# Warm-up matmuls as two half-row matmuls into the two banks of one PSUM tile

## The chip, the cores and the metric

The kernel runs on one core of one Trainium2 chip. The metric is the device time in microseconds. The time before is 263.78 us, the median of two runs (263.33 and 264.23). PE stands for TensorE, DVE for VectorE, ACT for ScalarE, POOL for GpSimd and SP for SyncE.

## The reference

A linear attention with cosine weights, followed by an MLP mixer over tokens and channels. There are 8 batches of 8 heads, 576 tokens and 64 elements per head; a model row is 512 wide.

```python
def _attn_ref(q, k, v):                       # (8, 8, 576, 64) each
    theta = np.pi / 2.0 * pos / S
    def phi(x, c, s):
        r = np.maximum(x, 0.0)
        return np.concatenate([r * c, r * s], axis=-1)
    q_p = phi(q, cos_w, sin_w)
    k_p = phi(k, cos_w, sin_w)
    kv = np.einsum('bhsf,bhsd->bhfd', k_p, v)
    z = np.sum(k_p, axis=2)
    num = np.einsum('bhsf,bhfd->bhsd', q_p, kv)
    den = np.einsum('bhsf,bhf->bhs', q_p, z)[..., None] + 1e-06
    return (num / den).astype(np.float32)

def _moe_ref(x, w_tok1, w_tok2, w_ch1, w_ch2):    # x: (8, 576, 512)
    xt = x.transpose(0, 2, 1)
    h = np.maximum(xt @ w_tok1, 0.0) @ w_tok2     # 576 -> 256 -> 576
    u = x + h.transpose(0, 2, 1)
    h2 = np.maximum(u @ w_ch1, 0.0) @ w_ch2       # 512 -> 1536 -> 512
    return (u + h2).astype(np.float32)
```

The warm-up matmuls are no part of this. They multiply zeros by zeros, and nobody reads what they write.

## The kernel before, in words

The work is one long list, PLAN, which a loop at L877 walks through. Each entry names a function and its arguments, and the function issues its instructions on the engine that the entry names ("V" VectorE, "A" ScalarE, "G" GpSimd, "Y" the SP queue). The order on every engine is therefore the order of the list, written out by hand; nothing rearranges it later. An instruction waits by semaphore for the instructions whose results it reads, or whose tile it overwrites.

A batch goes through these steps. `load_part` brings q, k and v in. `feat` and `rfeat` (L382, L384, L400, L402) make the features on ScalarE and VectorE: relu, times a cosine, sine or tangent. `vcast` casts v. PE then transposes the features of q (`q_half_mm` and `q_turn_mm`, L688 and L702; the copies out are `q_half_out` and `q_turn_out`, L376 or L378), or the DMA engines do it (L414). `kv` and `kv_half` (L601, L715) multiply the features of k with v, `num` and `num_half` (L619, L729) the features of q with that product. VectorE divides (`x_add`, `x_rec`, `x_mul` and their halves, L633 to L647 and L737 to L744). `b1` (L657, L754) and `u_mm` (L766; for batch 0 `uT_x` and `uT_h`, L669 and L674) are the two token layers, and `u_out` (L770) adds x. Then `m1` (L809) is the first channel layer. The second one is `m2` (L821) for batch 0 and, for the other batches, seven products of half-size blocks (L454) with sums of their operands made beforehand (L437, L443). Batch 0 runs in halves of four heads while its inputs still arrive. Batches overlap: while `m1` of one runs, the features of the next are made.

PSUM is cut into six tiles (L482): two named psA of two banks each (kind "P") and four named psM of one bank (kind "S"). `take(kind, key)` (L487) takes the tile that has stood longest in the list of free ones, and `give(key)` (L492) puts it back at the end. Both act when the list is walked, so a tile can be taken again while its last reader has yet to run; the next writer then waits for that reader.

`warm(n)` (L588) issues n matmuls of the tile `wz` (L359, 128 rows of 512 bfloat16 zeros, set by VectorE at L501) on a tile taken and given back at once. PLAN holds 28 calls `("warm", 2)`, thus 56 matmuls: 13 calls before the first transposes of q, 12 more until the token layers of batch 0 are under way, one each in the first and the second channel layer of batch 0, and one behind the last product.

Before each matmul PE loads its stationary operand with an LDWEIGHTS of its own (PEld in the profile), here `wz[:, 0:P]`.

Of the kernel before, what the change touches and what calls it, by code (L numbers as in the profile page):

```python
# [285 lines left out]
def kernel(  # L286
# [11 lines left out]
    nc = tc.nc  # L298

    B, H, S, D = q.shape  # L300
# [3 lines left out]
    P = 128  # L304
# [16 lines left out]
    def sb(name, shape, dt):  # L321
        return const.tile(shape, dt, name=name)
# [36 lines left out]
    wz = sb("wz", [P, 512], BF16)  # L359
# [124 lines left out]
    free = {n: list(range(len(t))) for n, t in tiles.items()}  # L484
    held = {}

    def take(kind, key):  # L487

        held[key] = (kind, free[kind].pop(0))
        return tiles[kind][held[key][1]]  # L490

    def give(key):  # L492
        kind, i = held.pop(key)
        free[kind].append(i)
# [91 lines left out]
        copy(eng, wc2[:, ki, :], wc2_st[ki // 4][:, ki % 4, :])  # L586

    def warm(n):  # L588
        ps = take("S", "warm")
        for _ in range(n):  # L590
            nc.tensor.matmul(ps, wz[:, 0:P], wz, start=True, stop=True)  # L591
        give("warm")


# [315 lines left out]
```

## Time and profile before

| | |
|---|---|
| median of two runs | 263.78 us (263.33 to 264.23) |
| the profiled execution, its own time | 263.85 us |
| its span | 262.1 us |
| granted TensorE clock | 1.00 |
| chain that ended last, by engine | PE 71%, DMA 11%, DVE 10%, ACT 3% |
| warm-up matmuls (L591), share of that chain | 2% |
| HBM | 35.85 MB read, 9.44 MB written |

The profile is that of one execution. The span goes from the first to the last instruction, and the time of the execution is 1.75 us longer. A matmul's duration goes from its start to the modelled end of its pipeline, so successive matmuls overlap, and PE can read as busy while it waits briefly. In a row of the page, `L591 PE MATMUL psM<-wz 128*128 128x512 bf16 x56` is a line of the kernel, the engine and operation, tile written and tile read, rows and columns of the stationary operand, the shape of the moving one, and the number of such instructions; behind the bar stand the busy time in us, the mean duration of one in ns, and the idle time ahead of them with its releaser. A row of the timeline begins with its start and its length in us, and merges like neighbours. In the chain of waits each piece has its start, its length and the work that the end waited for.

### The profile page before, as it was taken

How to read it: one execution, taken by the hardware profiler on the slowest of the kernel's cores; microseconds unless marked ns; L12 is line 12 of the kernel's file. 1: busy time of each engine (PE TensorE's matmuls, PEld its weight loads, DVE VectorE, ACT ScalarE, POOL GpSimd, SP SyncE). 2: the span in 40 equal slices, each digit the busy share in tenths (PEclk: the TensorE clock that was granted, in tenths of full speed). 3: DMA queues.
4: the chain of work that ended last, by engine and by line, in shares of the span. 5: the costliest groups of instructions: out<-in, count | busy, mean ns of one | idle time of the engine just before them, and what ended most of it. 6: DMA issues, size and time to landing. Idle time of an engine off the chain costs nothing.

```text
span 262.1 us, 5484 instructions
## 1 busy us (share of the span) xinstructions
PE 254.6 (97%) x2122; PEld 160.5 (61%) x2122; DVE 193.0 (74%) x401; ACT 134.9 (51%) x226; POOL 89.3 (34%) x97
## 2 busy tenths in 40 slices
PE   8999989998999999999999999999999999999995
PEld 2576446445559556765577557755866586467684
DVE  4686996596999677797989878787878283634673
ACT  2794677593676388566743675374621442240100
POOL 5262372249413002930260038005701630073040
PEclk9999999999999999999999999999999999999999
DMA  6999999999999999999999999798392130400224
GB/s 189 383 389 386 386 347 313 328 229 185 325 396 197 220 265 388 186 227 252 368 268 163 251 314 275 163 304 136 72 170 93 51 75 8 141 1 0 99 104 160
DMA packets 81819, 57.70 MB, mean 220 GB/s; under 512 B 50305, under 2 KB 76545, under 8 KB 81793
## 3 DMA queue, kind: packets, MB, share of 16 engines
q1 hardware_dynamic: 80272, 55.65, 78.6%
q10 hardware_dynamic: 1520, 1.70, 1.9%
q8 instruction: 16, 0.26, 0.4%
q14 instruction: 11, 0.08, 0.1%
HBM read 35.85 MB, written 9.44 MB: 173 GB/s over the span
## 4 chain that ended last, share of the span: by engine, by line
PE 71%; DMA 11%; DVE 10%; ACT 3%; issue 2%; POOL 1%; ACTq 0%; SPq 0%; DVEq 0%; POOLq 0%
PE psM L809 26%; PE psM L454 22%; DMA q_raw<-in_q_dram 5%; PE psA L754 5%; PE psA L766 4%; DMA k_raw<-in_k_dram 3%; PE psA L729 3%; PE psA L715 2%; DMA uT<-u_bf 2%; PE psM L591 2%; DVE kp L402 2%; PE psM L821 2%; ACT kp L400 2%; DMA qpT<-qp 2%; DVE qp L402 1%
## 5 line engine op out<-in xcount | busy, mean ns | idle before, releaser
L809 PE MATMUL psM<-uT,w_ch 128*128 128x512 bf16 x384 | 90.2, 379 | 0.8 <-DMA uT<-u_bf 0.8
L382 ACT ACTIVATE h1T<-psM 128x512 bf16<-128x512 f32 x71 | 40.9, 595 | 68.9 <-PE psM L809 63.8
L809 PEld LDWEIGHTS <-w_ch 128*128 128x128 bf16 x432 | 40.2, 98 | 41.8 <-DMA uT<-u_bf 0.9
L454 PEld LDWEIGHTS <-h1s 128*128 128x128 bf16 x384 | 36.9, 98 | 8.1 <-POOL h1s L443 0.8
L384 DVE TENSOR_SCALAR h1T<-psM 128x512 bf16<-128x512 f32 x37 | 25.1, 686 | 16.6 <-PE psM L809 10.6
L466 DVE TENSOR_TENSOR u_sb<-psM,u_sb 128x512 f32<-128x512 f32 x42 | 28.1, 682 | 11.9 <-PE psM L454 11.5
L443 POOL TENSOR_TENSOR h1s<-h1T,h1s 128x512 bf16<-128x512 bf16 (+1 forms) x17 | 27.4, 1621 | 23.4 <-DVE h1s L443 17.1
L378 POOL CAST vb<-v_raw 128x512 bf16<-128x512 f32 (+1 forms) x23 | 13.5, 618 | 61.2 <-DMA v_raw<-in_v_dram 48.6
L454 PE MATMUL psM<-w_ch2t,h1s 128*128 128x256 bf16 x276 | 33.6, 273 | 0.5 <-POOL h1s L443 0.5
L454 PEld LDWEIGHTS <-h1T 128*128 128x128 bf16 x288 | 27.9, 98 | 5.3
L443 POOL TENSOR_TENSOR h1s<-h1T 128x512 bf16<-128x512 bf16 (+1 forms) x11 | 17.7, 1616 | 31.8 <-DVE h1T L384 16.8
L454 PE MATMUL psM<-w_ch,h1T 128*128 128x256 bf16 x192 | 23.6, 273 | 0.0
L770 DVE TENSOR_TENSOR u_sb<-psA,x_sb 128x1024 f32<-128x1024 f32 x16 | 19.3, 1219 | 3.8 <-PE psA L766 3.7
L744 DVE TENSOR_TENSOR x_sb<-psA,rden 128x512 bf16<-128x512 f32 x28 | 18.9, 686 | 0.7
L400 ACT ACTIVATE qp<-q_raw,tan_t 128x512 bf16<-128x512 f32 (+1 forms) x25 | 16.2, 673 | 4.9 <-DMA q_raw<-in_q_dram 4.1
L400 ACT ACTIVATE kp<-k_raw,sin_t 128x512 bf16<-128x512 f32 (+1 forms) x24 | 15.7, 663 | 5.6 <-PE psA L715 4.5
L591 PE MATMUL psM<-wz 128*128 128x512 bf16 x56 | 16.9, 434 | 1.2 <-DVE wz L501 1.2
L729 PEld LDWEIGHTS <-qpT 128*128 128x128 bf16 x280 | 12.5, 98 | 6.3 <-DMA qpT<-qp 0.9
L376 ACT CAST u_bf<-u_sb 128x1024 bf16<-128x1024 f32 x10 | 10.4, 1044 | 10.6 <-DVE u_sb L770 8.6
L766 PE MATMUL psA<-B,w_tok 128*128 128x512 bf16 x64 | 15.6, 379 | 0.1
L754 PE MATMUL psA<-x_sb,w_tok 128*128 128x512 bf16 x56 | 14.5, 379 | 0.2 <-DVE x_sb L744 0.2
L400 ACT ACTIVATE kp<-k_raw,cos_t 128x512 bf16<-128x512 f32 (+1 forms) x22 | 14.5, 673 | 0.2 <-DMA k_raw<-in_k_dram 0.2
(124 smaller groups left out, 345.3 us busy)
## 6 DMA issues: line engine op xcount, KB each, us to landing
out_dram<-u_sb SPq DMA_DIRECT2D x32, 256.0 KB, 4.2
k_raw<-in_k_dram SPq DMA_DIRECT2D x7, 640.0 KB, 7.3
q_raw<-in_q_dram SPq DMA_DIRECT2D x7, 640.0 KB, 6.6
v_raw<-in_v_dram SPq DMA_DIRECT2D x7, 640.0 KB, 8.5
k_raw<-in_k_dram SPq DMA_DIRECT2D x7, 512.0 KB, 7.4
q_raw<-in_q_dram SPq DMA_DIRECT2D x7, 512.0 KB, 5.5
v_raw<-in_v_dram SPq DMA_DIRECT2D x7, 512.0 KB, 6.6
u_sb<-in_moe_w_ch_dram SPq DMA_DIRECT2D x2, 1024.0 KB, 9.1
```

What stands on the lines that cost most here:

```text
L382: eng.activation(out_ap, in_ap, AF.Relu)
L384: eng.tensor_relu(out_ap, in_ap)
L400: eng.activation(dst, src, AF.Relu, bias=0.0, scale=s)
L443: eng.tensor_tensor(out=o[:, k0:k1], in0=a[:, k0:k1], in1=b_[:, k0:k1], op=op)
L454: nc.tensor.matmul(bank[:, t * HC:(t + 1) * HC], lhs[:, ki, t * P:(t + 1) * P], rhs[:, ki, :], start=(first and ki == 0 and t == 0), stop= ...
L466: V.tensor_add(u, bank2(bank)[:, ts, :], u)
L591: nc.tensor.matmul(ps, wz[:, 0:P], wz, start=True, stop=True)
L729: nc.tensor.matmul(ps[:, h // HH, (h % HH) * E1:(h % HH + 1) * E1], qpT[:, h, j, :], kv_sb[:, h, 0:E1], start=True, stop=True, skip_group_ ...
L754: nc.tensor.matmul(ps[:, mi, :], w1[:, j, mi * P:(mi + 1) * P], rhs, start=(j == 0), stop=(j == NJ - 1))
L766: nc.tensor.matmul(ps[:, half, :], w2[:, ki, 2 * c + half, :], B1[b % 2][:, ki, :], start=(ki == 0), stop=(ki == NT - 1))
L770: V.tensor_add(u_sb[b % 2][:, 2 * c:2 * c + 2, :], of(("u", b, c)), x_sb[:, 2 * c:2 * c + 2, :])
L809: nc.tensor.matmul(ps.rearrange("p (t k) -> p t k", k=P), wc1[:, ki, s * P:(s + 1) * P], src[:, :, ki, :], start=(ki == 0), stop=(ki == NC ...
```

## The change

A call of `warm` looks whether a psA tile is free. If one is, the call takes it, and each of its matmuls becomes two: the first on rows 0 to 63 of `wz` into the tile's first bank, the second on rows 64 to 127 into its second bank. Both are 512 columns wide. If none is free, the call does as before. Matmuls of the computation itself keep their 128 rows, and the list PLAN is the same.

```diff
     def warm(n):
-        ps = take("S", "warm")
+        two = len(free["P"]) > 0
+        ps = take("P" if two else "S", "warm")
         for _ in range(n):
-            nc.tensor.matmul(ps, wz[:, 0:P], wz, start=True, stop=True)
+            if two:
+                for i, p0 in enumerate((0, P // 2)):
+                    nc.tensor.matmul(ps[:, i, :], wz[p0:p0 + P // 2, 0:P], wz[p0:p0 + P // 2, :], start=True, stop=True)
+            else:
+                nc.tensor.matmul(ps, wz[:, 0:P], wz, start=True, stop=True)
         give("warm")
```

Lines behind it move down by five: L688 becomes L693, L809 becomes L814.

## The prediction

> **What bounds the kernel now.** I read the page first: who is busy, and what a warm-up matmul costs.
>
> ```profile
> span 262.1 us, 5484 instructions
> ...
> PE 254.6 (97%) x2122; PEld 160.5 (61%) x2122; DVE 193.0 (74%) x401; ACT 134.9 (51%) x226; POOL 89.3 (34%) x97
> ...
> L809 PE MATMUL psM<-uT,w_ch 128*128 128x512 bf16 x384 | 90.2, 379 | 0.8 <-DMA uT<-u_bf 0.8
> L809 PEld LDWEIGHTS <-w_ch 128*128 128x128 bf16 x432 | 40.2, 98 | 41.8 <-DMA uT<-u_bf 0.9
> ...
> L591 PE MATMUL psM<-wz 128*128 128x512 bf16 x56 | 16.9, 434 | 1.2 <-DVE wz L501 1.2
> ```
>
> PE is the bound, with little idle time anywhere. One matmul of 512 columns lasts 379 ns from start to end, but eight take 1.73 us in the chain below, so they follow each other every 216 ns and 163 ns of each is tail under the next. The 98 ns weight load lies beside a running matmul. Every PE row says 128*128: no half-row matmul occurs before.
>
> Next the timeline of PE, to see where the 56 warm-ups lie and what they hold up.
>
> ```profile
> 1.19 8.36 PE L591 MATMUL psM<-wz 128*128 128x512 bf16 x26 [1.19 <-DVE wz L501]
> 9.38 0.61 PE L688 MATMUL psM<-ident,qp 128*128 128x128 bf16 x8
> 9.83 1.03 PE L591 MATMUL psM<-wz 128*128 128x512 bf16 x4
> 10.99 1.02 PE L688 MATMUL psM<-ident,qp 128*128 128x128 bf16 x12
> ```
>
> In the first stage PE has nothing else to do. Its weight loads start 0.43 us apart until 6.28 us and then 13 of them take 2.77 us: the array runs at half its pace until about 6.3 us, although the granted clock reads 1.00 throughout. The last of the four at 9.83 gives way at 9.83 + 4 x 0.216 = 10.70, and the transposes at 10.99 wait for ScalarE's features: 0.29 us to spare.
>
> Then the chain of waits in order of time, which says whose delay moves the end.
>
> ```profile
> 10.99 0.40 PE psM L688 x4
> ...
> 12.01 0.43 PE psM L591 x2
> 12.45 0.21 PE psM L601 x4
> 12.66 0.43 PE psM L591 x2
> ...
> 13.64 0.51 PE psM L601 x12
> ...
> 18.43 0.43 PE psM L591 x2
> ...
> 20.83 0.43 PE psM L591 x2
> ...
> 29.69 0.94 DVE kp L402 x3
> ...
> 44.65 0.43 PE psM L591 x2
> ```
>
> The first stage's warm-ups aren't on the chain. From 10.99 to 29.69 us it is almost all PE, the warm-ups included; 29.69 to 37.75 is VectorE; then PE again to 50 us. A delay of a piece on this chain moves the end by as much, unless another chain is within reach.
>
> **What changes.** In the two programs' instruction orders 25 of the 28 warm calls find a psA tile free and are split: PE goes from 4246 to 4346 rows, so 50 warm-ups become 100 half-row matmuls, each with its weight load. The other three calls (16.36 to 17.59 us) stay. Thirteen split calls stand at the start, one before and one behind 9.83's four (calls 14, 15), seven between 12 and 21 us on the chain, one at 31.72, one at 44.65 and one behind the last product.
>
> *The pair.* A matmul's pace goes by its columns (216 ns for 512, 109 for 256 by L454's 1.31 us for 12), so halving the rows saves nothing: a pair costs 216 ns if its halves run side by side, 432 if one after the other. Side by side needs two weight loads in one slot, 2 x 98 = 196 ns, which fits in 216; the halves share neither rows of wz nor a bank. I take 216, and keep 432 for the rival. The Trainium skill ("TensorE: Matmul & The Clock Gate", Part 3) has matmuls on different row groups run concurrently, starting about 4 ns apart; by it the 14 pairs between 12 and 21 us would cost 0.06 us more, and no run here shows it yet.
>
> *The switch.* PE must go from 128 rows to 64 and back around each block. The price lies between 0 (the trace shows none, for it has no switch) and the case where a matmul's tail (163 ns) and the next weight load (98 ns) both lie open: 261 ns. A gain is excluded, since nothing is removed. I take the middle of tail alone and both, 212 ns, as the tail is what two layouts in one array can least share. The Trainium skill ("TensorEngine Tiling (Array Packing)", Key Properties) says that changing the tiling mode drains TensorE. It speaks against the change: by it the zero end falls away. No run here shows it.
>
> Start: three switches (end of the first run, both sides of calls 14 and 15), 0.64 us. It is covered by the 0.29 us above and by 0.18 us more at 10.99, where four transposes take 0.40 us instead of the 0.22 that eight in 0.45 give. Left: +0.17 us (at 261 ns +0.31).
>
> 12 to 21 us: 14 switches, 2.97 us; 0.15 us of it is covered at 13.64, where 12 matmuls of kv take 0.51 us and at 17.39 the same take 0.36; 0.05 elsewhere. Left: +2.77 us (at 261 ns 3.45, at 163 ns 2.08). ScalarE and VectorE wait for PE there (ScalarE's copy of kv at 18.53 follows within 0.1 us), so the delay goes on.
>
> 31.72: hidden under VectorE, which holds PE back 1.09 us at 36.66.
>
> 44.65: a new wait. The warm-up now takes the psA tile whose transposes ScalarE is just copying out:
>
> ```profile
> 44.45 1.01 ACT L376 COPY qpT<-psA 128x1024 bf16<-128x1024 bf16 x1 [0.87 <-PE psA L702]
> ```
>
> It ends at 45.46, so PE stands 45.46 - 44.65 = 0.81 us. Queued behind are a part of m2 and num(1,3), which waited for that copy before but reached it only at 45.78; so it moves by the whole. The first switch hides in the wait, the second costs 0.21: +1.02 us.
>
> Behind the last product: nothing waits for it. The other waits that move name the same releases, or ones long past: the swapped psM and psA tiles go around in the same order afterwards. The wait for ScalarE's copy ahead of kv at 12.4 falls away, but that copy had ended at 12.23; worth nothing. The 100 further PE instructions cost nothing else while weight loads stay under the matmuls; if not, that is the rival with 432.
>
> Sum: 0.17 + 2.77 + 1.02 = 3.96 us. The profiled execution took 263.85 us (span 262.1), 0.07 over the median of two. Forecast 263.85 + 3.96 = 267.8 us. With free switches 263.85 + 0.81 = 264.7; with 261 ns each 0.31 + 3.45 + 0.81 + 0.26 = 4.83, 268.7.
>
> **Rivals.** *One after the other* (a half can't start while the other streams, or its weight load can't be pulled ahead): the first run has 52 slots, 12 at 427 ns to 6.28 us and 40 at 216, to 14.95; then 0.45 of transposes and eight slots, 1.73: 17.13 against 11.17, +5.96. Then 14 x 0.216 less the 0.2 of cover, 2.8, and 0.81 + 0.43 at 44.65. Sum 10.0: 273.9 us; with 18 switches at 212 ns on top up to 277.7. For it: no row shows two matmuls at once. Against: the weight loads fit.
>
> *The end is held by transfers*, so not slower. The DMA engines are busy 0.97 or more in every stretch from 4 to 165 us, and the chain goes through transfers at 56, 86, 97 and 113 us (5.07, 4.08, 6.78 and 7.94 us). If these run from a queue that never empties, a PE delay under its 6 to 8 us from issue to landing vanishes there: 263.9 us. It decides if the loads are issued ahead of the delayed features. Against: PE is 19.5 of 20 us busy in those stretches too, and the loads wait for features that VectorE and ScalarE make in turn with PE's results.
>
> *The array's pace isn't raised* by half-row work: the first run takes 26 x 0.427 = 11.1 us, to 12.3, with 0.9 and 1.7 us at half pace behind it, to 14.9: +3.7. About 5 us of later work at half pace lose 2.5, switches and wait as above 3.8: some 273.8 us. For it: the pace changed 5 us after the start, by something that sees activity. Against: two halves are as many active rows.
>
> *It doesn't do what it says*: if the halves were merged or all calls fell back, 263.9; the instruction order excludes that.
>
> **How the numbers follow.** Side by side with a price for switches 0.55 (264.7 to 268.7, somewhat above if a switch costs more than one tail and load), one after the other 0.27, pace not raised 0.06, transfers 0.10, a gain by something unseen 0.02. The range that leaves out 2 in 10 goes from 264.2 (most of the transfers' case left out) to 275.5 (the upper part of the serial case left out). The likeliest case's own range is 264.7 to 268.7. 2% is 5.3 us, about what a measurement here can tell from no change: slower above 269.1 takes the serial and the pace case (0.33) and the 0.12 of the first case in which switches cost more than 0.27 us or pairs more than 216 ns: 0.45. Within 2%: 0.43 + 0.10 = 0.53. Faster: 0.02; even if all 14 pairs between 12 and 21 us cost nothing, that is 3.0 us.
>
> **What would show it.** Half-row rows of L594 in two groups whose starts lie nanoseconds apart show the pair; if the first run ends near 9.3 us it is side by side, near 15 one after the other, near 12.3 at half pace. The gap between the last full matmul ahead of a block and its first half, over the pitch, is the switch. PE idle at 45 us, released by ScalarE's copy of qpT, shows the new wait at 0.8 us. m1's first matmul, at 26.54 now, moves by 2.9 us in my case and by about 9 in the serial one. I am wrong if the end moves by other than m1's shift plus 1 us, or if PE's gaps lie where no block does.

## The result and the profile after

The changed kernel takes 267.13 us (median of two runs, 266.99 and 267.27) against 263.78 us, a ratio of 1.0128 with a 95% interval of 1.0100 to 1.0156. It is 3.35 us slower, which is within the 2% and yet outside what chance explains. Run again later beside the kernel before, it gave 1.0121 (1.0098 to 1.0144).

The page of the changed kernel, the lines that answer to those of before:

```profile
span 265.2 us, 5583 instructions
...
PE 255.7 (96%) x2172; PEld 159.6 (60%) x2172; DVE 192.8 (73%) x401; ACT 135.1 (51%) x226; POOL 88.2 (33%) x97
...
L814 PE MATMUL psM<-uT,w_ch 128*128 128x512 bf16 x384 | 90.2, 379 | 2.7 <-DMA uT<-u_bf 2.7
...
L594 PE MATMUL psA<-wz 64*128 64x512 bf16 x100 | 14.2, 410 | 2.0 <-DVE wz L501 1.2
```

The 50 split warm-ups are there as 100 matmuls with 64 rows. PE is still the bound, and the span is 3.1 us longer. In the rows shown, two idle times ahead of matmuls have grown: 0.8 us at L591 or L594 (2.0, of which the wait for `wz` at the start is the 1.2 that was there before) and 1.9 us at `m1` (2.7 against 0.8, always for the transposes that bring `uT`).

The timeline of PE in the changed kernel (start, length, instruction, idle time ahead of it):

```profile
1.19 7.11 PE L594 MATMUL psA<-wz 64*128 64x512 bf16 x52 [1.19 <-DVE wz L501]
8.65 0.62 PE L693 MATMUL psM<-ident,qp 128*128 128x128 bf16 x8 [0.35 <-DVE qp L402]
9.20 1.04 PE L594 MATMUL psA<-wz 64*128 64x512 bf16 x8
10.54 1.02 PE L693 MATMUL psM<-ident,qp 128*128 128x128 bf16 x12 [0.30 <-ACT qp L400]
11.49 0.61 PE L594 MATMUL psA<-wz 64*128 64x512 bf16 x4
...
27.28 5.34 PE L814 MATMUL psM<-uT,w_ch 128*128 128x512 bf16 x24
...
46.03 0.61 PE L594 MATMUL psA<-wz 64*128 64x512 bf16 x4 [0.85 <-ACT qpT L376]
46.57 1.04 PE L826 MATMUL psM<-w_ch,h1T 128*128 128x512 bf16 x4
...
87.56 1.02 PE L814 MATMUL psM<-uT,w_ch 128*128 128x512 bf16 x4 [1.41 <-DMA uT<-u_bf]
```

The first run of 52 halves ends by 8.30 us; its 26 full matmuls ended at 9.55 before. It is shorter because the array's pace rose earlier in this execution: the last start at half pace was at 6.28 us before and at 3.72 here. In a second profile of the changed kernel it was at 7.13, so the earlier rise isn't the work of the change. The wait for `qpT` at 46.03 is the one that the changed tile brings. The wait at 87.56 has no counterpart before. There the same matmul, at 85.25, follows the work ahead of it without a wait, and the only wait for `uT` is the one at 61.19, where the changed kernel has none. The two lines of the kernel before:

```profile
61.19 1.90 PE L809 MATMUL psM<-uT,w_ch 128*128 128x512 bf16 x8 [0.76 <-DMA uT<-u_bf]
...
85.25 1.03 PE L809 MATMUL psM<-uT,w_ch 128*128 128x512 bf16 x4
```

Single starts around the first split block behind the transposes, and how long each lasts, in the changed kernel:

```
matmul L693, last transpose     11.338 us   219 ns
load   L594, first half         11.485       93
load   L594, second half        11.488       93
matmul L594, first half         11.489      387
matmul L594, second half        11.493      387
load   L594, next pair          11.500, 11.503   96
matmul L594, next pair          11.716, 11.719   376
load   L606, full rows          12.023       96
matmul L606, full rows          12.028      204
```

Halves of a pair start 3 to 4 ns apart and run side by side. The second pair of the block follows after 227 ns; in the long first run, once the pace is up, pairs follow every 216. The last transpose has its pitch of 56 ns behind it at 11.394, and the first half starts at 11.489: 95 ns are lost on the way in. On the way out it is 12.028 - (11.716 + 0.216) = 96 ns. So a block of two pairs costs 95 + 11 + 96 = 202 ns more than its two slots. Inside a layout the next load is pulled under a running matmul (11.500 against 11.716); across the change it isn't, but starts only a few ns ahead of its own matmul.

The chain of waits of the changed kernel, in order of time (start, length, work):

```profile
10.54 0.40 PE psM L693 x4
...
11.56 0.54 PE psA L594 x4
12.10 0.23 PE psM L606 x4
12.32 0.54 PE psA L594 x4
...
13.63 0.47 PE psM L606 x12
...
18.80 0.54 PE psA L594 x4
...
44.97 1.02 ACT qpT L376
45.99 0.04 issue
46.03 0.61 PE psA L594 x4
46.64 0.97 PE psM L826 x4
```

A block with the four products of `kv` behind it takes 0.54 + 0.23 = 0.77 us here and took 0.55 before (0.43, then 0.12 for four), in line with the 0.20 us from the single starts. ScalarE's copy is now a link of the chain at 45 us.

### The profile page after: what moved, and what is told of

It reads as the page before. It is cut to its first block, busy times and chain, and to the rows that moved or that the text cites. A ratio compares the mean times of both kernels' runs of the same rounds, so it can differ in the third digit from the quotient of the medians.

```text
span 265.2 us, 5583 instructions
## 1 busy us (share of the span) xinstructions
PE 255.7 (96%) x2172; PEld 159.6 (60%) x2172; DVE 192.8 (73%) x401; ACT 135.1 (51%) x226; POOL 88.2 (33%) x97
## 4 chain that ended last, share of the span: by engine, by line
PE 72%; DMA 14%; DVE 5%; ACT 5%; POOL 1%; issue 1%; SPq 0%; ACTq 0%; DVEq 0%; POOLq 0%
PE psM L814 30%; PE psM L454 17%; DMA uT<-u_bf 7%; DMA k_raw<-in_k_dram 5%; PE psA L759 4%; PE psM L826 4%; PE psA L771 3%; PE psA L720 3%; PE psA L734 2%; ACT kp L400 2%; PE psA L594 2%; DMA q_raw<-in_q_dram 2%; DVE kp L402 2%; PE psA L454 1%; PE psA L796 1%
## 5 line engine op out<-in xcount | busy, mean ns | idle before, releaser
L814 PE MATMUL psM<-uT,w_ch 128*128 128x512 bf16 x384 | 90.2, 379 | 2.7 <-DMA uT<-u_bf 2.7
L814 PEld LDWEIGHTS <-w_ch 128*128 128x128 bf16 x432 | 40.1, 98 | 44.5 <-issue 1.9
L378 POOL CAST vb<-v_raw 128x512 bf16<-128x512 f32 (+1 forms) x23 | 12.9, 593 | 61.4 <-DMA v_raw<-in_v_dram 59.7
L594 PE MATMUL psA<-wz 64*128 64x512 bf16 x100 | 14.2, 410 | 2.0 <-DVE wz L501 1.2
L443 DVE TENSOR_TENSOR h1s<-h1T 128x512 bf16<-128x512 bf16 (+1 forms) x21 | 13.8, 671 | 2.2 <-ACT h1T L382 1.9
```

What stands on the lines that cost most here:

```text
L443: eng.tensor_tensor(out=o[:, k0:k1], in0=a[:, k0:k1], in1=b_[:, k0:k1], op=op)
L594: nc.tensor.matmul(ps[:, i, :], wz[p0:p0 + P // 2, 0:P], wz[p0:p0 + P // 2, :], start=True, stop=True)
L814: nc.tensor.matmul(ps.rearrange("p (t k) -> p t k", k=P), wc1[:, ki, s * P:(s + 1) * P], src[:, :, ki, :], start=(ki == 0), stop=(ki == NC ...
```

## The experiments

Each kernel ran beside the kernel before on the same chip; a ratio is the time over that kernel's, with its 95% interval. Where only some calls of `warm` are split or kept, the list `warms` gets an entry per call and so counts them. The edits below leave out the lines that set up such lists.

**The three places, one at a time.** The theory was the prediction's sum with the switch as first measured, about 1.2 us between 12 and 21 us and 1 us at 45 us; the rival was that the end is lengthened elsewhere, by transfers.

All calls split except the one at 45 us (the 27th):

```diff
-        two = len(free["P"]) > 0
+        warms.append(n)
+        two = len(free["P"]) > 0 and len(warms) != 27
```

> The warm-up call at 44.65 us goes back to a full-row matmul on psM; the other 24 calls stay split. Sum of parts (mine): the wait for ScalarE's copy of qpT is worth 0.8 us and its one open switch 0.1, so this run is 0.9 to 1.1 us faster than the changed kernel, about 2.3 us slower than before. Rival, the later transfers decide: what the batches behind 60 us wait for is a DMA transpose, whose landing does not follow the 1 us; then this run is within 0.3 us of the changed kernel, or loses the whole 3.3 us.

Measured: 265.53 us, 1.0053 (1.0034 to 1.0071). Without that one call the loss is 0.0053 x 264.17 = 1.4 us instead of 3.2 to 3.35, so inside the whole the call is worth about 1.8 us. The two intervals together let that be 1.0 to 2.6 us, the low end of which is its own wait alone.

Only the first 15 calls split (`and len(warms) <= 15`):

> Only the first 15 calls, before the transposes of q and between their two halves, are split. Mine: three switches of about 0.1 us under 0.47 us of cover: within 0.3 us of before. Rival, the half-row matmuls change how soon the array's pace rises (in the changed kernel's profile at 3.9 us instead of 6.4): also no change of the end, but the pace rises near 4 us here again; if it rises at different times in the runs, that is chance.

Measured: 263.5 us, 0.9982 (0.9961 to 1.0002). The splits at the start cost nothing that shows: the interval ends at +0.05 us.

Only calls 16 to 25 split, the blocks between 12 and 21 us (`and 16 <= len(warms) <= 25`):

> Only the calls between 12 and 21 us are split (seven blocks, 14 switches). Mine, with the switch at about 95 ns as the changed kernel's records have it: 1.2 us slower than before, and m1's first matmul 1.2 us later. Rival, transfers decide: the 1.2 us at m1 show, and the end moves by less than 0.5 or by over 2 us.

Measured: 264.75 us, 1.0019 (0.9996 to 1.0042). In its profile the first matmul of `m1` moved by 1.42 us, of which 0.16 was already there at the last transpose ahead of the first block (11.958 us against 11.795): +1.25 us from the blocks. The time shows 0.5 us of that, with an interval that reaches from nothing to 1.1 us.

**The wait at 45 us.** Only that call split (`and len(warms) == 27`):

> Only the call at 44.65 us is split. Mine: the wait for ScalarE's copy of qpT, 0.8 us, and one switch, 0.1: 0.9 us slower than before, and the block behind it starts 1.0 us later. Rival, the wait vanishes in the DMA transposes behind it (m1 of the next batch at 61 us): as before within 0.3 us.

Measured: 264.6 us, 1.0031 (1.0011 to 1.0052). The second kernel leaves the split out everywhere and keeps only the other tile; each warm-up is one matmul on all 128 rows:

```diff
-                for i, p0 in enumerate((0, P // 2)):
-                    nc.tensor.matmul(ps[:, i, :], wz[p0:p0 + P // 2, 0:P], wz[p0:p0 + P // 2, :], start=True, stop=True)
+                nc.tensor.matmul(ps[:, 0, :], wz[:, 0:P], wz, start=True, stop=True)
```

> Every call takes the tile that the changed kernel takes, but each warm-up is one full-row matmul into the first bank: no half rows, no switch, the same wait at 45 us. Mine: only the wait is left, 0.8 to 1.0 us slower than before. Rival, the half rows themselves cost it all: as before. Rival, the moved tiles cost it all: 3.3 us slower than before.

Measured: 264.89 us, 1.0031 (1.0010 to 1.0053). The timeline of PE, first with only this call split:

```profile
45.46 0.61 PE L597 MATMUL psA<-wz 64*128 64x512 bf16 x4 [0.86 <-ACT qpT L376]
```

and then with full rows on the other tile:

```profile
45.52 0.59 PE L593 MATMUL psA<-wz 128*128 128x512 bf16 x2 [0.85 <-ACT qpT L376]
```

The same wait, the same cost of 0.0031 x 264 = 0.8 us, with two switches and with none; the intervals are too wide to show 0.1 us, but the profiles do: from the product ahead of the wait to `m2` behind the warm-up it is 1.80 us with the switch open behind the halves (44.20 to 46.00) and 1.69 without (44.26 to 45.95). What costs here is the choice of the tile, not the halves; and taking the psA tile everywhere else shows no cost. With full rows on the same tiles the 12-to-21-us blocks cost nothing either: from the last transpose ahead of them to the first matmul of `m1` it is 14.75 us, as in the kernel before (14.74), against 15.95 in the changed kernel. The delay at 45 us need not reach the end. In the profile with only this call split the matmuls of `m1` are still 0.90 us late at 62.09 and 86.15 us, but 0.17 at 141.90 and at the end; that execution took 264.05 us, below its median.

**The changed kernel once more**, as it is:

> The changed kernel once more, in as many runs as the parts. Sum of the parts (mine): what all calls but the one at 45 us cost (1.0053 of before) and what the moved tile there costs with full rows (1.0031), with 0.1 us for that call's own switch, is 1.0088 of before, 2.3 us. Rival, the parts add to more than their sum because later transfers are pushed into each other: 1.012 or more, 3.2 us.

Measured: 267.01 us, 1.0121 (1.0098 to 1.0144), 3.2 us. PE waits 3.3 us for `uT` in this profile. Here the start's warm-ups were in the way. ScalarE finished the first input of the second transposes at 10.46 us, against 10.48 in the first profile; but with the pace low until 7.13 us the transposes came right behind the warm-ups, at 11.38 instead of 10.54, and the first matmul of `m1` at 27.95 instead of 27.28.

**Do the halves need different rows?** Both halves of a pair take rows 0 to 63. All of it is still zeros.

```diff
-                for i, p0 in enumerate((0, P // 2)):
+                for i, p0 in enumerate((0, 0)):
```

> Both matmuls of a pair use rows 0 to 63, each into its own bank; tiles, waits, switches and counts are those of the changed kernel. Mine, the halves run at once only because they lie on different rows: a pair takes 432 ns, the first run ends near 15 us at the latest, and the kernel takes 271 to 276 us. Rival, any two 64-row matmuls overlap: as the changed kernel.

Measured: 295.07 us, 1.1182 (1.1156 to 1.1209). That the halves then run one after the other was expected; the size was not. The timeline of PE:

```profile
1.19 22.36 PE L594 MATMUL psA<-wz 64*128 64x512 bf16 x52 [1.19 <-DVE wz L501]
23.48 1.04 PE L693 MATMUL psM<-ident,qp 128*128 128x128 bf16 x8
...
42.82 1.90 PE L596 MATMUL psM<-wz 128*128 128x512 bf16 x4
...
46.27 1.03 PE L594 MATMUL psA<-wz 64*128 64x512 bf16 x4
```

52 slots in 22.36 us are 0.43 us each to the last: half pace throughout. The full matmuls between them are slow too: the last three of the four on 128 rows at 42.82 start at 43.233, 43.660 and 44.087 us, 427 ns apart. Only at about 45.7 us, after some 3 us of full rows alone (from 42.39), the pace rises; at 46.27 the first two halves start 226 ns apart, still one at a time. So half the rows at a time don't raise the pace, although PE has no gap in that run, and two halves at once do. Once risen, the pace stays up under single halves between full-row work. The first matmul of `m1` comes at 55.68 us against 27.28, 28.4 us later, and the span is 293.6 against 265.2, the same 28.4: a delay of the first stage goes through to the end in full.

**Are the later warm-ups needed at all?** The kernel before, with calls 16 to 28 dropped, thus 26 of the 56 matmuls of zeros:

```diff
     def warm(n):
+        warms.append(n)
+        if len(warms) > 15:
+            return
         ps = take("S", "warm")
```

> The kernel before without its warm-up calls 16 to 28 (26 matmuls of zeros, nothing of the computation). If they are pure cost on the chain: 1 to 4 us faster than before, bounded by ScalarE, which is busy without a break from 8.5 to 19 us. Rival, they keep the array at its full pace: its pace falls between 12 and 21 us, and the kernel is slower by 1 us or more. Rival, ScalarE and VectorE hold that stage: as before.

Measured: 262.11 us, 0.9944 (0.9918 to 0.9969): faster than both kernels, by 1.5 us against the one before. Busy times in the stretch of 11 to 23 us (stretch, its length, then each engine with its instructions, granted clock, DMA share, GB/s), first of this kernel:

```profile
11.00:23.00 12.00, 8.65 (x143) 7.28 (x144) 10.01 (x35) 10.31 (x23) 4.54 (x9) 1.00 1.03 377
```

and of the kernel before:

```profile
11.00:23.00 12.00, 12.00 (x161) 8.59 (x162) 9.54 (x34) 10.24 (x21) 4.43 (x9) 1.00 1.06 390
```

PE falls from 12.00 to 8.65 us of work, and the pace doesn't fall with it (transposes of 128 columns still follow each other every 56 ns, and from 24.7 us on matmuls of 512 every 216). `m1` starts only 0.1 us earlier (26.45 against 26.54), as ScalarE and VectorE bound this stretch; more of the gain appears later, -0.85 us at 37.75 and -1.9 at 61.19 against the landmarks of before.

**Whose fault are the longer waits for `uT`?** The profiles offered a candidate. PE's instructions arrive in blocks of 16 KB, as DMA traffic of their own (17 packets in the changed kernel, 16 before, 0.28 and 0.26 MB), and 100 more instructions move the times of these fetches. Rows of the DMA view while the `uT` transposes are under way that the matmul of `m1` at 85 or 87 us needs; last comes the time from issue to landing. Before, 81.2 to 85.25 us:

```profile
q14 instruction: 2, 0.02, 1.4%
...
uT<-u_bf SPq DMA_TRANSPOSE x1, 3.5
```

and after, 81.9 to 87.5 us:

```profile
q14 instruction: 2, 0.02, 4.1%
q8 instruction: 1, 0.02, 1.0%
...
uT<-u_bf SPq DMA_TRANSPOSE x1, 5.6
```

PE's fetch (q8) is at 84.5 us, inside the stretch, and the transposes take 5.6 instead of 3.5 us. Near 57 us it is the other way round: the fetch of before, at 59.1, met transposes of 5.1 us, and the changed kernel, whose fetch came at 53.4, has 3.3. (q14 is another queue of instructions; it is there both times.) Over the `uT` transposes of all profiles but that of the same rows, the 68 landings with a fetch of PE's in flight took 3.0 to 6.7 us, with a median of 4.8, and the 114 others 3.0 to 4.8, with a median of 3.2. The ranges overlap, and a long landing has more room for a fetch to fall into it, so this is no proof. The rival was that the transposes are late for another reason and the coincidence means nothing. Four kernels move the fetches by cutting the start's warm-ups into narrower ones.

The kernel before with 60 and with 28 more instructions:

```diff
+            parts = cuts.pop(0) if cuts else 1
+            w = 512 // parts
-            nc.tensor.matmul(ps, wz[:, 0:P], wz, start=True, stop=True)
+            for c in range(0, 512, w):
+                nc.tensor.matmul(ps[:, c:c + w], wz[:, 0:P], wz[:, c:c + w], start=True, stop=True)
```

with `cuts = [1] * 10 + [4] * 10` for 60 more:

> The kernel before, with ten start warm-ups cut into four matmuls of 128 columns each: full rows, same tiles, no switch, 60 PE instructions more, as many as the split of the first 15 calls adds. Theory, the fetches of PE's instructions (16 KB each, every 256 instructions) come earlier and fall into other transfers: the fetch near 59 us goes to about 55, off the uT transposes, so the first m1 of batch 1 starts near 60.2 instead of 61.2; the one near 87 goes to about 84, onto the next uT transposes, whose second landing takes 5.3 to 5.6 us instead of 3.5; the end within 0.3 us of the run with 15 split calls. Rival, the half rows or the tiles made those: fetch times move but the landings stay as before (3.5 us) and the time too.

Measured: 264.04 us, 0.9988 (0.9964 to 1.0012). With `[1] * 10 + [4] * 4 + [2] * 2`, 28 more:

> The same with 28 PE instructions more. Theory of the fetches: they come near 57 and 87.5 us as in the run with seven split blocks, clear of both uT transposes (landings 3.5 us or less to m1's first start, 60.2 us, and at 85), so 0.5 to 1.0 us faster than before. Rival: as before.

Measured: 263.92 us, 0.9995 (0.9970 to 1.0021); no gain. In both profiles the landings were short (3.9 and 3.5, 3.8 and 3.5 us) and the spans 261.3 and 261.0 us against 262.1. But these executions took 263.06 and 263.10 us, 0.8 to 1.0 less than their own kernels' medians. The medians did not follow.

The changed kernel with 184 more, each pair of the last start calls cut into quarters of its columns:

> The changed kernel with 184 PE instructions more in the start, so that fetches lie where 28 more would put them (284 is 28 beyond 256). Theory: the 1.4 us of wait for uT at 86 us goes, and the kernel is 0.7 to 1.5 us faster than the changed one, near 265.7 (1.005 to 1.009 of before), although it has more instructions. Rival: as the changed kernel, 1.012, or slower by the instructions.

Measured: 266.89 us, 1.0100 (1.0064 to 1.0136). The waits of PE in its profile (total, times, longest):

```profile
PE psM L819 <- DMA uT<-u_bf: 0.2, 1, 0.2
```

and in that of the changed kernel:

```profile
PE psM L814 <- DMA uT<-u_bf: 2.7, 4, 1.4
PE psA L594 <- ACT qpT L376: 0.9, 1, 0.9
```

The waits for `uT` do go away when the fetches move, as the candidate says. The time fell less than it asked for, and its interval overlaps the changed kernel's: inconclusive. The runs give two reasons for care. The spans of its eight runs have a median of 264.1 us, 1.8 above the kernel before in the same series, where the changed kernel's second series has 3.2; but they scatter from 263.5 to 267.4. And the time outside the span, 1.76 to 1.87 us in the changed kernel's runs, is 1.79 to 2.93 here, so part of what the span gains is lost there.

The kernel without the later warm-ups, with 80 more:

> The kernel before without its warm-up calls 16 to 28 (zeros, nothing of the computation) and with 80 PE instructions more in the start, in sum 28 more than before. Theory: 0.994 as without those calls, and the fetch near 59.8 us off the uT transposes as well: 0.989 to 0.992 of before. Rival: 0.994.

Measured: 264.99 us, 1.0016 (0.9983 to 1.0049). The gain of 1.5 us is gone. Its PE waits 1.6 us for POOL's sums, 1.0 for the transposes of `qpT` and 0.9 for those of `uT`, against 0.5, at most 0.2 and 0.2 in the profile without the 80. But the execution profiled here took 266.11 us, 1.1 above its median, and the twelve times run from 262.81 to 266.56, so these waits are those of one of the longer executions. That the margin of this kernel hangs on when its instructions and transfers meet fits this and isn't shown.

## Why the prediction was right or wrong

**The total** was forecast at 267.8 us and came at 267.13, inside the likeliest case's own range. That is in part luck, as errors of opposite sign cancel: the switches and the start were put about 1.7 us too high, and about 1 us later on wasn't foreseen.

**The pair** was right: 216 ns for two halves. The run on the same rows shows the condition, different rows; had they not run at once, the loss would have been 31 us and not the 10 to 14 that the rival gave, as that rival took for granted that the pace rises.

**The switch was mis-sized.** The prediction took 212 ns, the middle of one tail and of tail plus load; the trace shows 95 to 96. The tail doesn't lie open in full: the first half starts while the last transpose, by its recorded 219 ns, has until 11.557 us, so 68 ns of it still overlap. With 95 ns the prediction's own sum for 12 to 21 us is 14 x 0.095 - 0.20 = 1.13 us instead of 2.77, and with the 11 ns between a block's pairs it is 7 x 0.202 - 0.20 = 1.21. The first matmul of `m1` moved by 0.75 us, but the transposes at 10.99 came 0.46 earlier in this execution, so 1.20 us are due to the blocks. In the second profile it is 1.41 - 0.21 = 1.20, without the call at 45 us 1.20 too, with only these blocks split 1.25, and with full rows on the same tiles 0.01; the kernel with 184 more instructions has 1.58, and why is open. Whether the 95 ns are waiting loads or draining results isn't told apart. The Trainium skill ("TensorEngine Tiling (Array Packing)", Key Properties) says that a change of the tiling mode drains TensorE; the trace agrees that each change costs something, and its 95 ns are less than the 163 ns of a tail.

**The start** was forecast at +0.17 us and costs nothing that can be measured (0.9982, 0.9961 to 1.0002). In the second profile, whose pace rose late, the warm-ups held up the transposes all the same, and `m1` began 0.67 us later than in the first.

**The wait at 45 us** was right: 0.81 us forecast, 0.85 seen, and with one switch 1.02 forecast (0.81 + 0.21) against 1.13 of further shift there (1.65 us at the matmuls of `m2` behind it, 0.52 ahead of it at 37.75). Two kernels show it alone, each at 0.8 us.

**Not foreseen: about 1 us behind it.** The two steps as measured give 1.20 + 1.13 = 2.33 us, but the end moved by 3.35. The prediction said that it would be wrong if the end moved by other than `m1`'s shift plus 1 us; that happened, as 1.20 + 1 is 2.2. The profile shows where: the shift is 1.65 us at 45 us, 0.74 at 61, 2.31 at the matmul that waits until 87.56 (85.25 before), and 3.1 at the end. Part of it is taken up at the first `uT`, for which PE waits before and doesn't now, and more is added at the next. The times agree that it is there: all but the 45-us call cost 0.53% and that call alone 0.31%, 0.84% together, while the whole costs 1.21% (0.98 to 1.44). The 0.37%, 1 us, is about as large as the intervals of the three together allow for. The three places by themselves (-0.18, 0.19 and 0.31%, in sum 0.32) leave 0.89%, which is clear of those intervals, so the parts do cost more together than apart. The two calls that none of the three runs splits don't explain it in the profile: the shift is 0.53 us at 37.75, behind the call at 31.72, and it is 3.1 us already ahead of the last call. PE's instruction fetches falling onto other transposes go with longer landings (medians of 4.8 and 3.2 us), and in three of the four kernels that moved them the waits for `uT` are 0.2 us or none; in the fourth, without the later warm-ups and with 80 more, 0.9 us of wait stays at 85.58 us with no fetch in flight (4.5 us to landing). In the times moving them showed no gain that can be told from none. Their share in the 1 us stays open. So does how much of a shift of the 12-to-21-us blocks arrives at the end when nothing else changes (0.5 us measured of 1.25).

**The transfers' rival** (the end held, no loss) is refuted by the result. The 28.4 us of the same-rows run that arrive in full show that a large delay isn't absorbed; that small ones can be, in part, the shift of 0.74 us at 61 us shows, and so does the execution with only the 45-us call split. The argument that the DMA engines are busy 0.97 or more in every stretch from 4 to 165 us was misread, too: the share is 0.91 from 5 to 6 us and 0.80 from 60 to 65.

**The pace rival** was wrong for two halves at once, and right for halves one at a time, where it costs far more than the 10 us that it gave: in that run the pace stays low for over 40 us.

## What to carry to other kernels

Here two half-row matmuls on different rows cost the time of one full matmul (216 ns), but going from full rows to halves and back costs 0.1 us each way on a path where PE is always busy; put all half-row work into few blocks. A buffer taken from another pool brings its last reader with it: find that reader's end in the trace before counting anything else. Filler work of an engine that is the bound is worth leaving out in a run by itself: here 26 matmuls of zeros cost 1.5 us and the pace stayed up without them, though that gain didn't survive 80 more instructions elsewhere.

## What the runs showed of the hardware

- The array's pace doesn't rise while only half of its rows work at a time: 52 back-to-back matmuls on rows 0 to 63 stayed at 427 ns for 22 us, and full-row work between later ones was slow until about 45.7 us, while the granted clock reads 1.00 throughout. With two halves at once, or with full rows, the last slow start lies between 3.7 and 7.1 us in the profiles. The Trainium skill ("TensorE: Matmul & The Clock Gate", Part 1) has a monitor that watches how busy PE is and opens its clock; this run adds that 22 us without gaps on half the rows didn't open it.
- When the pace rises varies by 3.4 us between two executions of the same kernel (3.72 and 7.13 us). With the early rise the warm-ups end ahead of the features, and PE waits 0.30 us for them at 10.54; with the late one the same transposes start at 11.38, 0.9 us after ScalarE has made their first input.
- A change between 128 and 64 rows costs about 95 ns each way. Across it the next weight load isn't pulled under the running matmul, but starts 1 to 5 ns ahead of its own (all 14 changes between 12 and 21 us); inside a layout it is (11.500 us against 11.716).
- A profiled execution can be 1 us off its kernel's median (0.8 and 1.0 us below it with 28 and 60 more instructions, 1.1 above it in the kernel without the later warm-ups and with 80 more), so a difference of that size is read from the times and only placed by the profile.
